# Attention and gated MLP in one kernel: the planner's DMA durations are replaced by traced ones

## Chip, cores and metric

The kernel runs on one core of a Trainium2 chip. The metric is device time in microseconds; the time before is the median of three runs.

## The reference

Causal attention over 4 batches, 12 heads, 448 positions and a head width of 64, in float32; its output is laid out as 1792 tokens of 768 and goes through an MLP with a sigmoid gate.

```python
scores = q @ k.T / 8          # per head, masked above the diagonal with -1e9
attn = softmax(scores)
x = (attn @ v) -> reshaped to (1792, 768)
h = x @ w_in                  # (768, 2048)
g = h * sigmoid(1.702 * h)
out = g @ w_out               # (2048, 768), float32
```

## The kernel before

**Precision.** Most products are made of fp16 pairs: an operand is scaled and split into a high part (`scaled`, L476 on ScalarE or L478 on VectorE) and a rest (`rest`, L481, always VectorE), and three matmuls (high by high, high by rest, rest by high) replace one. The weights arrive as 64-bit numbers (16 loads of `w_in` at L652 and 16 of `w_out` at L704, 768 KB each) and are turned into float32 by the ScalarE and VectorE steps of `to_f32` (L570 to L603) before they are split. Six of the twelve heads' pairs of batch 0 use float32 for scores instead of splits.

**Blocks and units.** The work is cut into 8 blocks: each batch gives rows 0 to 255 (4 chunks of 64) and rows 256 to 447 (3 chunks). A block has 6 units, one for each pair of heads. A unit (`unit`) loads q (L856 for batch 0, L981 otherwise), transposes it (by TensorE at L870 for batch 0, else by a DMA transpose at L1040), makes scores (L1060, L1068), softmax (`chunk`, L1091 on VectorE and L1105 on ScalarE), splits the probabilities into `p`, transposes them by DMA into `PT` (L1179) and multiplies by v (L1197). Keys come at L936 and are transposed by DMA at L961; values come at L780. A `PT` transpose has 12 tiles in a 4-chunk block and 20 in a 3-chunk block; a `qT` transpose has 8 or 6, a `kT` transpose 14.

**MLP.** `h_slice` (L1268) multiplies a block's attention output `xT` by a slice of `w_in` into `ps_h`, gates it (L1289, L1294) and splits it into `gT`. `out_tile` (L1333) multiplies 128 tokens of `gT` by half of `w_out`, scales the result and stores it (L1357). `xT` is held for two blocks; `p`, `PT` and `qT` have two buffers each, `kf` and `qf` one.

**The order of instructions.** Nothing runs as the loops read. Every piece of work is put into a list, `Ops`, with a cost on each engine that can do it, what it reads and writes, a due time (`prio`, from `TUNE`) and, for a DMA, the time `dma` that it takes on the bus. `Ops.order` then simulates the list forward, engine by engine, and takes the order in which the simulation issued; for an operation that two engines can do, it takes the engine too. It repeats this 300 times from one random seed, with due times that a backward simulation yields and that random numbers disturb, and keeps the order with the best simulated score. All DMAs go through the one queue of SyncE. The simulation gives a DMA this time:

```python
go = max([now] + flying[-self.DMA_DEPTH :][: len(flying) // self.DMA_DEPTH][:1])
free[e] = go + costs[e]
bus = max(bus, go + self.DMA_START) + dma
end = bus + self.DMA_END
```

A DMA with `dma` over 1.0 (weights, v, all transposes) is "bulk": it is held back while the simulated bus is more than `TUNE["slack"]`, 5.13 us, behind. `scored` and `late` rate an order with random delays, and use the same constants.

Of the kernel before, what the change touches and what calls it, by code (L numbers as in the profile page):

```python
# [59 lines left out]
class Ops:  # L60
# [9 lines left out]
    HOP = 0.14  # L70
    SECOND = 1e5
    LOAD = 0.68
    DMA_START, DMA_END, DMA_DEPTH = 1.0, 0.8, 8
    ROWS = 0.19

    def __init__(self):
        self.ops = []
# [244 lines left out]
def kernel(  # L322
# [13 lines left out]
    P = 128  # L336
# [25 lines left out]
    vraw = cp.tile([P, NJ, H, D], F32, name="vraw")  # L362
# [411 lines left out]
    def v_batch(b, prio):  # L774
        st = bst[b]
        for j in range(NJ):
            r = min(P, S - j * P)
            add(
                {"SP": Ops.LOAD},
                lambda e, j=j, r=r: nc.sync.dma_start(  # L780
                    out=vraw[:r, j], in_=v[b, :, j * P : j * P + r, :].rearrange("h p d -> p h d")
                ),
                [], [("vraw", j, 0)] + ([("vraw", j, 1)] if r == P else []), prio, dma=2.18 * r / P,
            )
        sqv, sqv_key = col("sqv", 2, 2 * NJ)
        sq, sq_key = col("sqv1", 2)
        if b == 0 and TUNE["gram_v"]:
            x = vraw.rearrange("p j h d -> p j (h d)")
            for j in range(NJ):
                gram(  # L790
                    x[:, j : j + 1], [("vraw", j, h) for h in range(2)], ps_o[1], ("O", 1), j == 0, j == NJ - 1, prio
                )
            gram_max(ps_o[1], ("O", 1), sq, sq_key, prio)
        for j in range(2 * NJ if not (b == 0 and TUNE["gram_v"]) else 0):
            square_sum(
                NU * D, junk(NU * D).rearrange("p (h d) -> p h d", d=D), [],
                vraw[:, j // 2, j % 2 * NU : j % 2 * NU + NU], [("vraw", j // 2, 0), ("vraw", j // 2, 1)],
                sqv[:, j : j + 1], (sqv_key, j), prio,
            )
        if not (b == 0 and TUNE["gram_v"]):  # L800
            add(
                dve(2 * NJ),
                lambda e: nc.vector.tensor_reduce(out=sq, in_=sqv, axis=AX.X, op=ALU.max),
                [(sqv_key, j) for j in range(2 * NJ)], [sq_key], prio,
            )
        amx, amx_key = all_max(sq, sq_key, "v", "S" if b else "O", prio)
        st["s_v"], st["s_v_key"] = col("s_v", 2)
        st["i_v"], st["i_v_key"] = col("i_v", 2)
        norm_scale("v", amx, amx_key, st["s_v"], st["s_v_key"], st["i_v"], st["i_v_key"], prio)
# [41 lines left out]
    def load_heads(dst, src, r, keys, prio, dma):  # L851

        for j in range(2):
            add(
                {"SP": Ops.LOAD},
                lambda e, j=j: nc.sync.dma_start(  # L856
                    out=dst[:r, j], in_=src[j].rearrange("(p t) d -> p t d", p=r)
                ),
                [], keys[j], prio, dma=dma,
            )  # L860
# [16 lines left out]
    def k_unit32(u, c0, c1, prio):  # L877

        m = u % 2
        f = q16[:, m * 16 * D : m * 16 * D + 8 * D].bitcast(F32).rearrange("p (j t d) -> p j t d", j=2, d=D)  # L880
        w = 64 * (c1 - c0)
        r = w // 2
        keys = [("q16", m, j) for j in range(4)]
        load_heads(f, k[0, 2 * u : 2 * u + 2, 64 * c0 : 64 * c1], r, [keys[:2], keys[2:]], prio, 0.045 * (c1 - c0))
        got, got_key = turn(f, r, keys, prio)
        kt = kT[u // 2][:, u % 2 * NC : u % 2 * NC + NC].rearrange("p c w -> p (c w)").bitcast(F32)
        add(
            {**act(w, psum=True, rate=1.2), **dve(w, rate=1.2)},
            lambda e: scaled(e, kt[:, 64 * c0 : 64 * c1].rearrange("p (x t) -> p x t", t=2), got, 1.0),
            [got_key], [("kT", u, c) for c in range(c0, c1)], prio,  # L890
        )
        bst[0]["kT", u] = kt

    def q_unit32(n, u, prio):
        b, c0, c1 = blocks[n]
        ni = c1 - c0
        i = u % 2
        r = 32 * ni
        f = qf[:, i].rearrange("p (j t) d -> p j t d", j=2)
        keys = [("qf", i, j) for j in range(2)]  # L900
        load_heads(f, q[b, 2 * u : 2 * u + 2, 64 * c0 : 64 * c1], r, [[x] for x in keys], prio, 0.045 * ni)
        got, got_key = turn(f, r, keys, prio)
        t = qT_r.next()
        qt = qT[t].rearrange("p c w -> p (c w)").bitcast(F32).rearrange("p (c j w) -> p c j w", j=2, w=64)
        key = ("qT", t)
        if stale[t]:
            stale[t] = False
            for j in range(2):
                add(
                    {"POOL": 0.4},  # L910
                    lambda e, j=j: nc.gpsimd.memset(qt[64 * j : 64 * j + 64, :, 1 - j], 0.0), [], [key], prio - 1,
                )
        for j in range(2):
            add(
                {**act(64 * ni, psum=True, rate=1.0), **dve(64 * ni)},
                lambda e, j=j: scaled(
                    e,
                    qt[64 * j : 64 * j + 64, :ni, j].rearrange("p c (x t) -> p c x t", t=2),
                    got[64 * j : 64 * j + 64].rearrange("p (c x) t -> p c x t", c=ni),
                    1.0,  # L920
                ),
                [got_key], [key], prio,
            )
        return qt[:, :ni], key, -QK_SCALE, None

    def k_pair(b, u, prio):
# [4 lines left out]
        for a in range(2):  # L931
# [29 lines left out]
            lambda e: nc.sync.dma_start_transpose(out=t, in_=flat),  # L961
            [("k16", 0), ("k16", 1)], [("kT", u + a, c) for a in range(2) for c in range(NC)], prio - TUNE["tr"], dma=2 * NC * Ops.ROWS,
        )
# [4 lines left out]
    def q_pair(n, u, prio):  # L968

        b, c0, c1 = blocks[n]  # L970
        ni = c1 - c0
        w = 64 * ni

        f = qf.rearrange("p u c d -> p (u c) d")[:, : 2 * ni]
        keys = []
        for a in range(2):
            for j in range(2):
                keys += [("qf", a, j)]
                add(
                    {"SP": Ops.LOAD},  # L980
                    lambda e, a=a, j=j: nc.sync.dma_start(  # L981
                        out=f[64 * j : 64 * j + 64, a * ni : (a + 1) * ni],
                        in_=q[b, 2 * (u + a) + j, 64 * c0 : 64 * c1].rearrange("(c p) d -> p c d", p=64),
                    ),
                    [], keys[-1:], prio, dma=0.09 * ni,
                )
        sq, sq_key = col("sqq", 2)
        square_sum(
            2 * w, junk(2 * w).rearrange("p (x d) -> p x d", d=D), [], f, keys, sq, sq_key, prio
        )  # L990
        (s, s_key), (inv, inv_key) = col("s_q", 2), col("i_q", 2)
        norm_scale("q", sq, sq_key, s, s_key, inv, inv_key, prio)
        ik, ik_key = bst[b]["ik", u]
        c, c_key = col("c", 3)
        add(
            tiny(1),
            lambda e: by(e).tensor_scalar(
                out=c, in0=inv, scalar1=-QK_SCALE, scalar2=ik, op0=ALU.mult, op1=ALU.mult
            ),
            [inv_key, ik_key], [c_key], prio,  # L1000
        )
        h = q16[:, : 8 * w].rearrange("p (x g h d) -> p x g h d", g=2, h=2, d=D)

        def part(g):
            return [("q16", a, g) for a in range(2)]

        add(
            {**act(2 * w, ap=1), **dve(2 * w, ap=1, rate=0.521)},
            lambda e: scaled(e, h[:, :, 0, 0], f, s),
            keys + [s_key], part(0), prio,  # L1010
        )
        add(
            dve(2 * w, ap=1),
            lambda e: rest(h[:, :, 0, 1], f, s, h[:, :, 0, 0]),
            keys + [s_key] + part(0), part(1), prio,
        )
        for g in range(2):

            def dup(e, g=g):
                dst, src = h[:, :, 1, 1 - g], h[:, :, 0, g]  # L1020
                if e == "DVE":
                    nc.vector.tensor_copy(dst, src)
                else:
                    nc.gpsimd.tensor_scalar(out=dst, in0=src, scalar1=1.0, scalar2=1.0, op0=ALU.mult, op1=ALU.mult)  # L1024

            add({**pool(2 * w, 0.84), **dve(2 * w, rate=0.26)}, dup, part(g), part(2 + g), prio)
        bst[b]["c", n] = c, c_key
# [106 lines left out]
    def unit(n, u, prio):  # L1134
# [15 lines left out]
        for i0 in range(c0 - c0 % 2, c1, 2):  # L1150
# [32 lines left out]
            [("p16", pp_i, x, g) for x in range(ne) for g in range(2)], all_keys, prio - TUNE["tr"],  # L1183
            dma=2 * Ops.ROWS * ne,
        )
# [276 lines left out]
```

## Time and profile before

| | |
|---|---|
| time, median of 3 runs | 640.23 us (637.7 to 640.47) |
| profiled execution | span 633.9 us from the first to the last instruction; its own device time is not listed beside the three runs |
| instructions | 14759 |
| PE busy | 582.6 us, 92% |
| DVE / ACT / POOL busy | 422.4 / 357.2 / 96.6 us |
| SyncE's DMA queue | 62.7% of 16 engines' span |

Read it in stages: an engine's share of the whole span says little, since the first 160 us and the rest have different limits.

### The profile page before, as it was taken

The numbers are of one execution on the slowest core, as the hardware profiler recorded it, in microseconds if no ns is written. First come the engines' busy times: TensorE is split into PE (matmuls) and PEld (weight loads), VectorE is DVE, ScalarE is ACT, GpSimd is POOL, SyncE is SP. The second block draws the span as 40 slices with busy tenths as digits, with TensorE's granted clock in tenths as the row PEclk, the third lists the DMA queues.
The fourth block names the chain that finished last, engine by engine and source line by source line (L and its number), as shares of the span: only waits on it lengthen the run. The fifth ranks groups of instructions, "written<-read, shape, count | busy, mean of one in ns | idle before, by whom it ended". The sixth has DMA issues, their size and how long they took to land. (4 is left out here: it accounts for less than half of the span.)

```text
span 633.9 us, 14759 instructions
## 1 busy us (share of the span) xinstructions
PE 582.6 (92%) x5723; PEld 439.5 (69%) x5723; DVE 422.4 (67%) x1128; ACT 357.2 (56%) x835; POOL 96.6 (15%) x235
## 2 busy tenths in 40 slices
PE   4777688978999999998999999999999999999997
PEld 3555466754588767876678667885679688777964
DVE  4999899999978898977498976769644213101300
ACT  4878888778657776758465565557343223012210
POOL 2233220043202124121021521001000000000000
PEclk9976689999999999999999999999999999999999
DMA  8999969678599687999847798627620040000000
GB/s 276 271 277 293 220 224 284 194 188 166 110 176 190 120 164 124 180 159 173 176 103 135 136 181 160 127 62 130 122 67 2 13 96 1 3 26 26 1 26 26
DMA packets 226407, 85.71 MB, mean 135 GB/s; under 512 B 207137, under 2 KB 216097, under 8 KB 226337
## 3 DMA queue, kind: packets, MB, share of 16 engines
q1 hardware_dynamic: 226336, 84.76, 62.7%
q8 instruction: 45, 0.74, 0.5%
q14 instruction: 26, 0.20, 0.1%
HBM read 41.68 MB, written 5.51 MB: 74 GB/s over the span
## 5 line engine op out<-in xcount | busy, mean ns | idle before, releaser
L1268 PE MATMUL ps_h<-xT,wib 128*128 128x192 f16 (+1 forms) x2304 | 239.3, 261 | 3.5 <-DVE gT L481 3.4
L1333 PE MATMUL ps_o<-wob,gT 128*128 128x384 f16 (+1 forms) x1536 | 233.8, 326 | 5.3 <-DVE wob L481 2.3
L1268 PEld LDWEIGHTS <-wib 128*128 128x128 f16 x2304 | 207.0, 98 | 31.8 <-issue 12.1
L1333 PEld LDWEIGHTS <-gT 128*128 128x128 f16 (+1 forms) x1536 | 131.4, 101 | 87.0 <-issue 12.6
L1105 ACT ACTIVATE z<-z,cols 128x320 f32<-128x320 f32 (+5 forms) x168 | 83.8, 500 | 47.1 <-DVE cols L1091 40.1
L1294 DVE SCALAR_TENSOR_TENSOR ps_h<-t,ps_h 128x512 f32<-128x512 f32 (+1 forms) x64 | 39.9, 624 | 76.5 <-ACT t L1289 76.3
L481 DVE SCALAR_TENSOR_TENSOR p<-z,cols,p 128x384 f16<-128x384 f32 (+3 forms) x168 | 82.6, 523 | 3.0 <-ACT p L476 1.9
L1091 DVE CUSTOM_DVE_ANT_0 z<-ps_s,mask,cols 128x384 f32<-128x384 f32 (+6 forms) x126 | 55.8, 478 | 30.1 <-PE ps_s L1068 30.1
L1289 ACT ACTIVATE t<-ps_h,cols 128x512 f32<-128x512 f32 (+1 forms) x64 | 40.1, 627 | 60.0 <-PE ps_h L1268 59.5
L476 ACT ACTIVATE p<-z,cols 128x128 f16<-128x128 f32 (+3 forms) x108 | 55.3, 538 | 15.4 <-DVE cols L1169 6.7
L1163 POOL TENSOR_SCALAR cols<-cols 128x2 f32<-128x2 f32 (+1 forms) x70 | 20.1, 287 | 208.6 <-ACT z L1105 207.7
L481 DVE SCALAR_TENSOR_TENSOR gT<-ps_h,gT 128x512 f16<-128x512 f32 (+1 forms) x64 | 39.6, 620 | 15.8 <-ACT gT L476 15.7
L476 ACT ACTIVATE gT<-ps_h 128x512 f16<-128x512 f32 (+1 forms) x58 | 31.1, 539 | 28.3 <-DVE ps_h L1294 28.1
L476 ACT ACTIVATE ob<-ps_o,cols 128x384 f32<-128x384 f32 x23 | 13.2, 575 | 59.8 <-PE ps_o L1333 59.8
L1197 PEld LDWEIGHTS <-v 128*64 128x64 f16 x864 | 38.4, 113 | 9.6 <-issue 7.6
L1197 PE MATMUL ps_v<-PT,v 128*64 128x192 f16 (+3 forms) x864 | 41.1, 243 | 4.1 <-DMA PT<-p 4.1
L1068 PE MATMUL ps_s<-kT,qT 128*64 128x192 f16 (+4 forms) x504 | 38.8, 277 | 2.4 <-DVE cols L1091 1.3
L1060 PE MATMUL ps_s<-kT,qT 128*128 128x64 f32 (+6 forms) x84 | 29.3, 468 | 2.6 <-DVE cols L1091 1.9
L1024 POOL TENSOR_SCALAR q<-q 128x512 f16<-128x512 f16 (+1 forms) x30 | 25.2, 841 | 43.0 <-ACT q L476 30.1
L1105 ACT ACTIVATION_READ_ACCUMULATOR z<-z,cols 128x1 f32 x168 | 31.7, 188 | 0.0
L476 ACT ACTIVATE wob<-wob 128x768 f32<-128x768 f32 (+1 forms) x19 | 20.8, 1095 | 15.6 <-DMA wob<-in_moe_w_in_dram 10.6
L1068 PEld LDWEIGHTS <-qT 128*64 128x64 f16 x504 | 19.6, 110 | 13.9 <-issue 9.9
(89 smaller groups left out, 541.1 us busy)
## 6 DMA issues: line engine op xcount, KB each, us to landing
wob<-in_moe_w_in_dram SPq DMA_DIRECT2D x16, 768.0 KB, 6.0
wob<-in_moe_w_out_dram SPq DMA_DIRECT2D x9, 768.0 KB, 5.5
vraw<-in_moe_w_out_dram SPq DMA_DIRECT2D x7, 768.0 KB, 5.4
out_dram<-ob SPq DMA_DIRECT2D x28, 192.0 KB, 2.1
vraw<-in_v_dram SPq DMA_DIRECT2D x12, 384.0 KB, 5.7
kf<-in_k_dram SPq DMA_DIRECT2D x36, 112.0 KB, 2.9
qf<-in_q_dram SPq DMA_DIRECT2D x48, 64.0 KB, 3.2
qf<-in_q_dram SPq DMA_DIRECT2D x48, 48.0 KB, 2.7
```

Of the source, the lines that this page charges most:

```text
L476: nc.scalar.activation(out=dst, in_=src, func=AF.Copy, scale=sc)
L481: nc.vector.scalar_tensor_tensor(out=dst, in0=src, scalar=sc, in1=hi, op0=ALU.mult, op1=ALU.subtract)
L1024: nc.gpsimd.tensor_scalar(out=dst, in0=src, scalar1=1.0, scalar2=1.0, op0=ALU.mult, op1=ALU.mult)
L1060: nc.tensor.matmul(ps, qt[:, i - c0].rearrange("p j w -> p (j w)"), kt[:, : 64 * (i + 1)], start=True, stop=True)
L1068: nc.tensor.matmul(ps[64 * j : 64 * j + 64], qt[:, g, i - c0, 64 * j : 64 * j + 64], kt[:, : i + 1, 64 * j : 64 * j + 64], start=(g == 0), ...
L1091: lambda e: nc.vector.tensor_tensor_reduce(out=z[:, :w], in0=ps, in1=mask[:, S - w :], scale=c, scalar=3.0e38, op0=ALU.add, op1=ALU.min, a ...
L1105: lambda e: nc.scalar.activation(out=z[:, :w], in_=z[:, :w], func=AF.Exp, bias=m, scale=-1.0, accum_out=l),
L1197: nc.tensor.matmul(ps[64 * j : 64 * j + 64, 64 * (first - c0) : w], vt[:, gv, J, j, :], PT[pi][:, at, gp, 64 * j : 64 * j + 64], start=(t ...
L1268: nc.tensor.matmul(ph[:, t], wib[:, sl, u, gw, t * P : (t + 1) * P], xT[x][:, gx, u, :w], start=(u == 0 and gw + gx == 0), stop=(u == NU - ...
L1289: lambda e: nc.scalar.activation(out=th, in_=ph, func=AF.Tanh, scale=ts[:, sl : sl + 1]),
L1294: lambda e: nc.vector.scalar_tensor_tensor(out=ph, in0=th, scalar=1.0, in1=ph, op0=ALU.add, op1=ALU.mult),
L1333: nc.tensor.matmul(po[o : o + m, :OH], gT[:, f, gg, 64 * r : 64 * r + m], wo_pair(f, gw, nh), start=(f == 0 and gg + gw == 0), stop=(f == ...
```

## The change

Durations in the planner's simulation are replaced: the fixed time ahead of a transfer from 1.0 to 1.23 us and behind it from 0.8 to 0.95 us, a tile of a DMA transpose from 0.19 to 0.214 us, a 128-row load of v from 2.18 to 2.43 us, a q or k load of batch 0 from 0.045 to 0.062 us per chunk, a later q load from 0.09 to 0.125 us per chunk. Those of the weights (2.2), later k loads (0.64) and stores (0.6) stay. No instruction, buffer or due time in `TUNE` changes; what can change is the order of instructions on each engine, and which of two engines takes an operation.

```diff
-    DMA_START, DMA_END, DMA_DEPTH = 1.0, 0.8, 8
-    ROWS = 0.19
+    DMA_START, DMA_END, DMA_DEPTH = 1.23, 0.95, 8
+    ROWS = 0.214
...
-                [], [("vraw", j, 0)] + ([("vraw", j, 1)] if r == P else []), prio, dma=2.18 * r / P,
+                [], [("vraw", j, 0)] + ([("vraw", j, 1)] if r == P else []), prio, dma=2.43 * r / P,
...
-        load_heads(f, k[0, 2 * u : 2 * u + 2, 64 * c0 : 64 * c1], r, [keys[:2], keys[2:]], prio, 0.045 * (c1 - c0))
+        load_heads(f, k[0, 2 * u : 2 * u + 2, 64 * c0 : 64 * c1], r, [keys[:2], keys[2:]], prio, 0.062 * (c1 - c0))
...
-        load_heads(f, q[b, 2 * u : 2 * u + 2, 64 * c0 : 64 * c1], r, [[x] for x in keys], prio, 0.045 * ni)
+        load_heads(f, q[b, 2 * u : 2 * u + 2, 64 * c0 : 64 * c1], r, [[x] for x in keys], prio, 0.062 * ni)
...
-                    [], keys[-1:], prio, dma=0.09 * ni,
+                    [], keys[-1:], prio, dma=0.125 * ni,
```

## Rows read from the trace of the kernel before

**Rows 1.** The page: span, busy time, and PE and its granted clock in 40 slices.

```profile
span 633.9 us, 14759 instructions
...
PE 582.6 (92%) x5723; PEld 439.5 (69%) x5723; DVE 422.4 (67%) x1128; ACT 357.2 (56%) x835; POOL 96.6 (15%) x235
...
PE   4777688978999999998999999999999999999997
...
PEclk9976689999999999999999999999999999999999
```

**Rows 2.** By stretch: length; busy PE, PEld, DVE, ACT, POOL; PEclk, DMA share, GB/s.

```profile
0.00:20.00 20.00, 10.53 (x66) 8.28 (x67) 10.65 (x26) 11.46 (x22) 4.91 (x22) 1.00 0.90 280
20.00:100.00 80.00, 60.05 (x504) 45.16 (x505) 74.39 (x178) 66.23 (x138) 22.68 (x39) 0.81 1.01 256
100.00:160.00 60.00, 51.14 (x465) 36.64 (x464) 57.32 (x117) 48.92 (x93) 14.45 (x30) 1.00 0.84 202
160.00:200.00 40.00, 37.04 (x414) 28.76 (x413) 34.41 (x106) 26.13 (x71) 7.34 (x16) 1.00 0.81 153
200.00:300.00 100.00, 98.19 (x1131) 75.36 (x1129) 85.77 (x263) 70.75 (x194) 21.34 (x56) 1.00 0.90 157
300.00:500.00 200.00, 195.36 (x1949) 146.63 (x1949) 138.79 (x409) 108.22 (x278) 25.91 (x73) 1.00 0.58 111
500.00:634.00 134.00, 130.34 (x1203) 98.64 (x1201) 21.07 (x34) 25.51 (x44) 0.00 (x0) 1.00 0.10 26
```

**Rows 3.** DMA issues of the first 100 us: count, KB, median us to landing.

```profile
q<-in_k_dram SPq DMA_DIRECT2D x12, 64.0 KB, 5.1
qf<-in_q_dram SPq DMA_DIRECT2D x12, 64.0 KB, 4.8
q<-in_k_dram SPq DMA_DIRECT2D x12, 48.0 KB, 4.3
qf<-in_q_dram SPq DMA_DIRECT2D x12, 48.0 KB, 5.0
...
PT<-p SPq DMA_TRANSPOSE x7, 7.1
```

**Rows 4.** DMA issues from 200 to 300 us.

```profile
vraw<-in_v_dram SPq DMA_DIRECT2D x3, 384.0 KB, 5.2
qf<-in_q_dram SPq DMA_DIRECT2D x12, 64.0 KB, 2.7
qf<-in_q_dram SPq DMA_DIRECT2D x12, 48.0 KB, 2.2
...
qT<-q SPq DMA_TRANSPOSE x12, 3.2
PT<-p SPq DMA_TRANSPOSE x12, 4.9
vraw<-in_v_dram SPq DMA_DIRECT2D x1, 192.0 KB, 7.1
kT<-k SPq DMA_TRANSPOSE x3, 4.4
```

**Rows 5.** Waits of PE, whole span: total us, times, longest.

```profile
PE ps_o L870 <- DMA q<-in_k_dram: 10.8, 4, 8.4
...
PE ps_v L1197 <- DMA PT<-p: 4.1, 3, 3.0
```

**Rows 6.** Waits of PE from 160 us to the end.

```profile
PE ps_s L1068 <- DMA qT<-q: 1.2, 2, 1.0
PE ps_v L1197 <- DMA PT<-p: 1.2, 2, 0.8
```

**Rows 7.** Waits of ACT in the first 160 us.

```profile
ACT wob L476 <- DMA wob<-in_moe_w_in_dram: 10.6, 7, 3.4
...
ACT wob L476 <- DMA wob<-in_moe_w_out_dram: 5.0, 5, 1.9
```

**Rows 8.** PE's timeline from 72 us: start, duration, operation.

```profile
72.63 3.25 PE L1268 MATMUL ps_h<-xT,wib 128*128 128x256 f16 x18
```

## Prediction

> **What bounds the kernel now.** The page comes first: PE is busy for 582.6 of 633.9 us, and its row of slices shows that what it lacks lies at the left end, where the granted clock falls too [rows 1]. So the kernel has to be read by stretches [rows 2]. From 160 us to the end PE is busy for 37.04 + 98.19 + 195.36 + 130.34 = 460.9 of 474 us at full clock: 13.1 us idle in all, and no order can win more than that there. In the first 160 us it is busy for 121.7 us, idle for 38.3 us, and from 20 to 100 us the mean granted clock is 0.81, that is, part of the time at 1.2 instead of 2.4 GHz. In this stretch VectorE is busy for 74.39 of 80 us and the DMA share is full (1.01): PE waits there for operands that VectorE, ScalarE and the transfers make ready. The MLP's first matmul stands at 72.63 us [rows 8]; before it PE has only attention and small helper matmuls, whatever their order.
>
> The waits tell how much of this is a transfer's doing. Over the whole span PE waits 10.8 us for loads of k and q, 8.4 of them for the first load of all, which nothing can precede, and 4.1 us for PT [rows 5]. From 160 us on, waits for DMAs are 1.2 + 1.2 = 2.4 us [rows 6]. ScalarE waits for weights, 10.6 + 5.0 us early on [rows 7].
>
> **The change part by part.** It adds and removes no instruction and no transfer; every duration of a single instruction keeps its row. What it moves is the order, by what the planner now thinks of DMAs. So the question is whether the new numbers are nearer to the trace, and what follows from the error where they are not.
>
> *A single transfer, late.* From 200 to 300 us the 64 KB q load lands 2.7 us after its issue, the 48 KB one 2.2 us [rows 4]. The planner's old time without a queue is 1.0 + 0.36 + 0.8 = 2.16 and 2.07 us, its new one 1.23 + 0.5 + 0.95 = 2.68 and 2.56 us: nearer for the one, too long for the other. A qT transpose lands in 3.2 us; old 1.8 + 0.19 x 8 = 3.32 or (6 tiles) 2.94 us, new 2.18 + 0.214 x 8 = 3.89 or 3.46 us. A PT transpose lands in 4.9 us; old 1.8 + 0.19 x 12 = 4.08 or (20 tiles) 5.60, mean 4.84; new 4.75 or 6.46, mean 5.60 us. A kT transpose lands in 4.4 us; old 1.8 + 14 x 0.19 = 4.46, new 5.18 us. So for transposes the old numbers fit the late stretch and the new ones are about 0.5 to 0.8 us too long.
>
> *A single transfer, early.* The small loads of the first 100 us land in 4.3 to 5.1 us and PT in 7.1 us [rows 3]. The old numbers without a queue are 1.98 us and 4.08 us, the new ones 2.43 and 4.75 us: both are short of it, and the new ones less so, since the real time contains a full bus. In this stretch the change is toward the trace.
>
> *The bus, early.* In the first 100 us the planner's demand grows by 12 x 2 x 4 x 0.017 = 1.63 us for the 64 KB loads, 12 x 2 x 3 x 0.017 = 1.22 us for the 48 KB ones, (6 x 12 + 20) x 0.024 = 2.21 us for seven transposes [rows 3], and 3.5 x 0.25 = 0.88 us for the v of batch 0 by the code: 5.9 us. The weights themselves keep 2.2 us, but they are bulk and are held while the simulated bus is over 5.13 us behind, so they are what is pushed: in the planner's order their loads, and the conversions on VectorE and ScalarE that follow, stand up to 5.9 us later beside attention work. On the chip the bus was full already, so no byte moves slower; what may come later is the MLP's first matmul. Bounds: nothing, if the order of weights stays, and 5.9 us, if the whole push arrives at PE. From below a gain is not excluded: ScalarE's 15.6 us of waiting for weights [rows 7] can shrink if their users are put later and other work before them. What that can bring is bounded by VectorE's idle time in 20 to 100 us, 80 - 74.39 = 5.6 us [rows 2], because VectorE is what the stretch runs on. I take a loss of half the push, 3.0 us: nothing in the rows tells more of the order, and a VectorE at 93% leaves little to fill.
>
> *The bus, late.* From 200 to 300 us the demand grows by 6 x 32 x 0.024 = 4.61 us for PT (half of each size), 6 x 14 x 0.024 = 2.02 for qT, 3 x 14 x 0.024 = 1.01 for kT, 12 x 0.14 + 12 x 0.105 = 2.94 for q and 0.88 for v [rows 4]: 11.5 us. The traced share there is 0.90 [rows 2], so the planner now sees a bus at about 101% and spreads attention over up to 11.5 us more in this stretch. The work that hides it is the MLP of the blocks before, at PE: it was 98.19 us busy of 100 with attention paced by the old numbers, and the last stretch has 130 us of PE work with the bus nearly empty (0.10) as reserve. Bounds: a gain of the 2.4 us of DMA waits [rows 6] on the one side, 11.5 us on the other, if `xT` of the next block is late where no MLP work is left. I take 0.5 us, the mean of what the idle shares of PE in the rows on either side make of 11.5 us (1.8% from 200 to 300 us: 0.2; 7.4% from 160 to 200 us: 0.85).
>
> *The rest of the edit* (stores and later k loads pay only the longer fixed times, 0.38 us each) is hidden by the same reserve; without cover it would be one such time at the last store, and that one is after the end of planning.
>
> Sum for the span: 633.9 + 3.0 + 0.5 = 637.4 us. The median of the runs stands 6.3 us above the profiled span, so 643.7 us. Half a per cent, 3.2 us, is about what can be told from no change here: the three runs before differ by 2.8 us.
>
> **The rivals.**
>
> *Order changes, time does not* (30%, 640.2 us). For it: 474 of 634 us are PE-bound with 2.4 us of DMA waits, so durations of transfers decide nothing there, and early the bus is full under either set of numbers. Against it: the planner searches with random disturbances and compares scores, so one constant suffices to pick another order and other engine choices in the first 160 us, where 38 us of PE time are open.
>
> *Faster* (29%). The planner now expects the small loads later, puts their users behind other ready work, and ScalarE and VectorE stop waiting in line. If half of VectorE's 5.6 us of idle time is filled, and half of the 2.4 us late, the time is 640.2 - 2.8 - 1.2 = 636.2 us. It decides if more than 3.2 us of VectorE's holes between 20 and 100 us close. Within these 29%, 4% are for more than this: at the full clock the 60.05 us of PE work of that stretch would take 60.05 x 0.81 = 48.6 us, 11.4 us less, and the time would be 628.8 us. That PE waits there on VectorE speaks against it: a shorter matmul then only waits longer. The Trainium skill (TensorE: Matmul & The Clock Gate, section HAM oscillation) states that waits for DMA between bursts of matmuls bring the clock back down each time, so that a removed wait would pay twice; the trace shows the low clock where such waits are, but more of PE's holes there end on VectorE.
>
> *Slower by starvation late* (9%, 640.2 + 11.5 = 651.7 us). Attention, spread by the planner's full bus, hands over `xT` so late that the MLP runs dry; two blocks of `xT` are all the stock there is. From 160 to 200 us PE was 7.4% idle, so the stock can be thin. It decides once PE falls below about 95% between 200 and 500 us. Against it: PE's 98.19 us.
>
> *The change does nothing at all*: only if the search lands on the same order; with every DMA's landing shifted by at least 0.38 us I give it no share of its own; it would end in the 30%.
>
> **How the numbers follow.** The likeliest case is the push of weights early (32%, 643.7 us, by its bounds 640.2 to 646.1 plus the 0.5). With starvation that makes slower 41%, no change 30%, faster 29%. The range reaches below to 640.2 - 5.6 - 2.4 = 632.2 us, all of VectorE's holes early and all DMA waits late, and above to both losses together with two thirds of the late one, 640.2 + 5.9 + 7.6 = 653.7 us; outside lie the clock case and a full starvation. I give 632 to 654 us; the likeliest one's own range is 640 to 647 us.
>
> **What would show it.** Right: the first MLP matmul stands later than 72.6 us, by 1 to 6 us, PE's busy time before 160 us falls below 121.7 us, and from 200 to 500 us PE stays above 97%; waits of PE for qT and PT late fall under 2.4 us, since the planner is now too careful. Wrong step early: the first MLP matmul stands earlier, or VectorE is over 95% busy from 20 to 100 us. Wrong step late: PE below 95% from 200 to 500 us. The forecast is wrong as a whole if the new order differs mostly by chance: then PE's idle time before 160 us moves by several us with no tie to the weights' loads or to DMA waits.

## The result and the profile after

The changed kernel is faster: 628.84 us (median of 4 runs, 628.13 to 629.87) beside 639.23 us (637.7 to 640.47), a ratio of 0.9855 with a 95% interval of 0.982 to 0.9891. The forecast was 643.7 us and slower; the range began at 632.

The page of the changed kernel: span, busy time, PE and its clock in 40 slices, and then the chain that ended last.

```profile
span 626.4 us, 14747 instructions
...
PE 583.0 (93%) x5723; PEld 438.8 (70%) x5723; DVE 415.4 (66%) x1105; ACT 363.5 (58%) x848; POOL 98.3 (16%) x245
...
PE   2767689798999999999999999999999999999997
...
PEclk9967789899999999999999999999999999999999
...
PE 59%; DVE 2%; ACT 0%; issue 0%; DVEq 0%; ACTq 0%
```

PE has the same work as in [rows 1], 583.0 us for 582.6. The 7.5 us between the two spans are PE's holes, and from the second quarter on its row is nines. The chain, where it can be followed back, is nearly all PE's, and no transfer is in it. The profiled run took 628.13 us beside its span of 626.4, so only 1.7 us lie around a span: by that measure the profiled execution of the kernel before took about 635.6 us, some 4.6 us less than its median of 640.23, and the 6.3 us that the prediction put on top of the span were mostly that. So the traces show 7.5 us of the 10.4 us by which the medians differ; the rest is not seen in them.

By stretch, the columns as in [rows 2]:

```profile
0.00:20.00 20.00, 7.21 (x46) 5.48 (x48) 7.50 (x15) 10.76 (x19) 4.52 (x21) 1.00 1.02 263
20.00:100.00 80.00, 60.22 (x510) 45.12 (x507) 77.75 (x187) 68.58 (x142) 23.58 (x41) 0.79 0.97 261
100.00:160.00 60.00, 54.73 (x500) 39.88 (x499) 58.74 (x129) 53.05 (x101) 16.03 (x34) 0.97 0.84 208
160.00:200.00 40.00, 38.66 (x410) 29.08 (x408) 32.66 (x98) 26.06 (x71) 6.98 (x18) 1.00 0.96 177
200.00:300.00 100.00, 99.37 (x1123) 75.71 (x1121) 80.56 (x243) 71.13 (x195) 18.01 (x51) 1.00 0.81 148
300.00:500.00 200.00, 200.00 (x2001) 150.23 (x1999) 136.62 (x402) 109.85 (x281) 29.16 (x81) 1.00 0.61 110
500.00:634.00 134.00, 122.84 (x1149) 93.31 (x1147) 21.57 (x35) 24.03 (x42) 0.00 (x0) 1.00 0.11 24
```

Before 160 us PE is busy for 122.2 us, with [rows 2] 121.7: nothing won, nothing lost. From 160 us to the end it is idle for 626.4 - 160 - 460.9 = 5.5 us, before for 13.0 (633.9 - 160 - 460.9). From 300 to 500 us it has no hole at all, where it had 4.6 us. In both kernels 3.6 us of this idle time lie behind PE's last matmul, while the last results are scaled and stored; what an order could win were the other 9.4 us, and 2.0 us of them are left. So the whole gain lies in the PE-bound stretch, where the prediction put a loss of 0.5 us.

What PE waits for there, first in the kernel before (the longest, beside [rows 6]), then in the changed one, the whole list:

```profile
PE ps_h L1268 <- DVE gT L481: 2.3, 3, 1.4
PE ps_o L1333 <- DVE ob L478: 1.6, 1, 1.6
PE ps_s L1068 <- DVE cols L1091: 1.3, 2, 1.0
```

```profile
PE ps_o L1333 <- DVE wob L481: 1.3, 2, 0.9
PE ps_s L430 <- DVE cols L1091: 0.5, 1, 0.5
PE ps_s L1068 <- DVE cols L1091: 0.2, 1, 0.2
```

No DMA is left in it. The idle time fell by more than the 2.4 us of [rows 6], because transfers also stood further back behind PE's waits. ScalarE's waits for DMAs from 160 us on, in the kernel before (those over 2 us) and then in the changed one:

```profile
ACT waste L466 <- DMA qf<-in_q_dram: 8.5, 8, 2.0
...
ACT k L466 <- DMA kf<-in_k_dram: 5.6, 2, 4.2
...
ACT p L476 <- DMA PT<-p: 2.2, 2, 1.4
...
ACT q L476 <- DMA qT<-q: 2.1, 5, 0.8
```

```profile
ACT waste L466 <- DMA qf<-in_q_dram: 5.6, 5, 2.9
...
ACT q L476 <- DMA qT<-q: 5.6, 4, 2.8
...
ACT k L466 <- DMA kf<-in_k_dram: 0.9, 1, 0.9
```

ScalarE stood in its queue for q and k, and the exponentials, splits and MLP steps behind it were late for VectorE and so for PE. The chain of the kernel before shows such links from a load of q to a wait of PE (for `gT` at 333.57 us, for `cols` at 358.80 us). Start, duration, what:

```profile
325.06 2.24 DMA qf<-in_q_dram
327.40 0.35 ACT waste L466
...
328.01 0.65 ACT z L1105 x2
328.67 0.37 ACT gT L476
329.04 0.55 ACT z L1105 x2
...
333.05 0.48 DVE gT L481
333.57 0.90 PE ps_h L1268 x9
...
343.70 3.18 DMA qf<-in_q_dram
346.99 0.12 ACT waste L466
...
358.21 0.52 DVE z L1091
358.80 0.46 PE ps_s L1068 x4
```

PE stood for 0.60 us before the first of these two matmuls and for 0.95 us before the second. The two longest holes lie ahead of this chain, and the timeline shows the same there. Before the 1.40 us for `gT` that end at 193.34 us, ScalarE had stood for 1.41 us for a PT and then for 0.78 us for a q load, and VectorE's queue behind it. Before the 1.58 us for `ob` that end at 301.41 us, ScalarE had stood for 0.80 us for a load of v, and VectorE then for 2.35 us for ScalarE's `z`, which came behind the work on v, with `ob` behind it in VectorE's queue. How much of each hole the transfer alone made is not told by this (of the last at most 0.80 us). The sum of ScalarE's waits for DMAs is no measure of PE's holes, though: it is 20.0 us here and 12.1 us in the changed kernel, but 19.5 us in `latency`, a run below whose idle time from 160 us on is 7.0 us. So it matters which of them reach PE.

The q loads and the transposes are no faster. From 200 to 300 us in the changed kernel, to be held against [rows 4]:

```profile
qf<-in_q_dram SPq DMA_DIRECT2D x12, 64.0 KB, 2.8
qf<-in_q_dram SPq DMA_DIRECT2D x12, 48.0 KB, 2.3
...
PT<-p SPq DMA_TRANSPOSE x11, 5.0
qT<-q SPq DMA_TRANSPOSE x10, 3.2
```

And the MLP's first matmul is later than in [rows 8], 81.1 us for 72.6 (line, engine, count, duration ns, first and last start):

```profile
L1268 PE MATMUL ps_h<-xT,wib x31: 269/394/421, 81.1 to 89.0; 128*128 128x256 f16 x31
```

### The profile page after: what moved, and what is told of

It is laid out like the page before. It is cut to its first block, busy times and chain, and to the rows that moved or that the text cites. A ratio compares the mean times of both kernels' runs of the same rounds, so it can differ in the third digit from the quotient of the medians.

```text
span 626.4 us, 14747 instructions
## 1 busy us (share of the span) xinstructions
PE 583.0 (93%) x5723; PEld 438.8 (70%) x5723; DVE 415.4 (66%) x1105; ACT 363.5 (58%) x848; POOL 98.3 (16%) x245
## 4 chain that ended last, share of the span: by engine, by line
PE 59%; DVE 2%; ACT 0%; issue 0%; DVEq 0%; ACTq 0%
PE ps_o L1333 28%; PE ps_h L1268 25%; PE ps_s L1068 4%; PE ps_v L1197 3%; DVE z L1091 0%; DVE gT L481 0%; DVE v L481 0%; DVE ps_h L1294 0%; DVE k L481 0%; DVE p L481 0%; DVE p L478 0%; DVE q L481 0%; ACT ob L476 0%; DVE xT L481 0%; PE ps_s L430 0%
## 5 line engine op out<-in xcount | busy, mean ns | idle before, releaser
L1091 DVE CUSTOM_DVE_ANT_0 z<-ps_s,mask,cols 128x320 f32<-128x320 f32 (+6 forms) x126 | 55.9, 478 | 29.3 <-PE ps_s L1068 28.9
L476 ACT ACTIVATE p<-z,cols 128x384 f16<-128x384 f32 (+3 forms) x118 | 60.7, 542 | 14.7 <-DVE cols L1169 13.6
L1163 POOL TENSOR_SCALAR cols<-cols 128x2 f32<-128x2 f32 (+1 forms) x79 | 28.4, 360 | 221.0 <-ACT z L1105 219.8
L1197 PEld LDWEIGHTS <-v 128*64 128x64 f16 x864 | 36.5, 111 | 8.5 <-issue 6.1
L1068 PE MATMUL ps_s<-kT,qT 128*64 128x64 f16 (+4 forms) x504 | 38.7, 277 | 0.2 <-DVE cols L1091 0.2
L1060 PE MATMUL ps_s<-kT,qT 128*128 128x64 f32 (+6 forms) x84 | 30.9, 503 | 6.2 <-ACT qT L476 3.6
L1024 POOL TENSOR_SCALAR q<-q 128x512 f16<-128x512 f16 (+1 forms) x27 | 20.9, 777 | 56.3 <-ACT q L476 47.8
```

Source lines behind the costliest of these rows:

```text
L476: nc.scalar.activation(out=dst, in_=src, func=AF.Copy, scale=sc)
L1060: nc.tensor.matmul(ps, qt[:, i - c0].rearrange("p j w -> p (j w)"), kt[:, : 64 * (i + 1)], start=True, stop=True)
L1068: nc.tensor.matmul(ps[64 * j : 64 * j + 64], qt[:, g, i - c0, 64 * j : 64 * j + 64], kt[:, : i + 1, 64 * j : 64 * j + 64], start=(g == 0), ...
L1091: lambda e: nc.vector.tensor_tensor_reduce(out=z[:, :w], in0=ps, in1=mask[:, S - w :], scale=c, scalar=3.0e38, op0=ALU.add, op1=ALU.min, a ...
L1163: lambda e, ls=ls: by(e).tensor_scalar(out=ls, in0=ls, scalar1=1e-9, scalar2=2.0**-14, op0=ALU.add, op1=ALU.mult),
L1197: nc.tensor.matmul(ps[64 * j : 64 * j + 64, 64 * (first - c0) : w], vt[:, gv, J, j, :], PT[pi][:, at, gp, 64 * j : 64 * j + 64], start=(t ...
```

## The experiments

Two numbers are read from each profile. **Late idle** is the span less 160 us less PE's busy time from 160 us on. **First part** is the span less the late idle, that is, 160 us plus the PE work still to do then; a good start makes it small. Ratios are against the kernel before, timed on the same chip.

| run | transfers of batches 1 to 3 planned | ratio (95%) | span | late idle | first part |
|---|---|---|---|---|---|
| before | old | 1 | 633.9 | 13.0 | 620.9 |
| after | new | 0.9855 (0.982 to 0.989) | 626.4 | 5.5 | 620.9 |
| old_seed3 | old | 0.9994 (0.997 to 1.002) | 632.4 | 12.9 | 619.5 |
| old_seed5 | old | 0.9974 (0.995 to 1.000) | 631.6 | 13.6 | 618.0 |
| new_first | old | 1.0015 (0.999 to 1.004) | 635.8 | 12.3 | 623.5 |
| short_later | shorter | 1.007 (1.003 to 1.011) | 640.0 | 24.6 | 615.4 |
| latency | fixed times new | 0.9861 (0.982 to 0.990) | 623.5 | 7.0 | 616.5 |
| rows | transposes new | 0.9891 (0.986 to 0.992) | 627.9 | 8.5 | 619.4 |
| loads | loads new | 0.988 (0.985 to 0.991) | 627.1 | 8.5 | 618.6 |
| new_seed3 | new | 0.9852 (0.981 to 0.989) | 624.5 | 5.4 | 619.1 |
| new_seed5 | new | 0.9955 (0.992 to 0.999) | 631.6 | 6.2 | 625.4 |
| new_later | new | 0.9821 (0.978 to 0.986) | 621.4 | 5.1 | 616.3 |
| new_later_seed3 | new | 0.9871 (0.983 to 0.991) | 628.4 | 5.6 | 622.8 |
| double | doubled step | 1.0013 (1.000 to 1.003) | 635.6 | 8.3 | 627.3 |
| double_seed3 | doubled step | 1.001 (0.999 to 1.003) | 635.0 | 8.8 | 626.2 |
| double_later | doubled step | 0.9936 (0.992 to 0.996) | 631.0 | 8.4 | 622.6 |
| double_later_seed3 | doubled step | 0.9833 (0.979 to 0.987) | 626.7 | 5.6 | 621.1 |
| hop | old | 0.9865 (0.984 to 0.989) | 627.8 | 10.0 | 617.8 |

**Where it was won: two orders joined.** Both orders are planned, the first 886 of 2845 operations (to about 160 us) are taken from one, the others from the other.

```diff
-        return best[1]
+        head = made[EARLY][:CUT]          # made[0]: old durations, made[1]: new; CUT = 886
+        taken = {i for i, _ in head}
+        return head + [x for x in made[1 - EARLY] if x[0] not in taken]
```

> The first 886 of 2845 operations in the order of the kernel before (about to 160 us), all others in the order and on the engines of the changed kernel. If the gain was made late (PE's idle time from 160 us on went from 13.1 to about 5.5 us, that of the first 160 us stayed at 38 us), the time is within 2 us of the changed kernel's 629, ratio 0.983 to 0.988. If it was made early, it is within 2 us of 639.

> The other way round: the changed kernel's order for the first 886 operations, then that of the kernel before. If the gain was made late: 637 to 641 us, with PE's idle time from 160 us on back at 10 to 14 us. If early: 628 to 631 us.

Neither came out: 635.45 us, ratio 0.9988 (0.9966 to 1.001), and 634.95 us, 0.9979 (0.9954 to 1.0005). The first met a seam. From 160 to 200 us, and its longest late wait of PE (its lines stand 11 further down than the kernel before's):

```profile
160.00:200.00 40.00, 33.23 (x352) 24.52 (x351) 28.79 (x85) 23.11 (x59) 6.83 (x15) 0.91 0.80 163
```

```profile
PE ps_s L441 <- ACT k L477: 5.5, 1, 5.5
```

PE lost 6.8 us at the joint, of which 5.5 in one wait, and the granted clock was 0.91 there. PE's work took 586.6 us, but from 20 to 100 us, ahead of the joint, the clock was lower too (0.77 for 0.81). Behind 200 us the idle time goes with the later order: 4.6 us with the new one (changed kernel 4.2), 8.6 us with the old one (kernel before 10.0). The times are no verdict, the holes only a hint; hence the other way of parting it below.

**Is it a mere draw of the search? Other seeds.**

```diff
-SEED = 2
+SEED = 3          # 3 and 5, with the old and with the new durations
```

> The kernel before with another random seed (3 for 2) and its old durations. If the durations themselves made the gain (an order planned with longer transfers leaves room for them), this stays at 636 to 645 us, with DMA waits of PE late. If the gain was another draw of the random search, this is as likely to be at 629 as at 640.

> The changed kernel with seed 3 for 2. If the durations made the gain: 625 to 632 us, PE's idle time from 160 us on under 8 us, no DMA waits of PE over 1 us there. If it was the draw: anywhere from 628 to 645 us.

> The kernel before with seed 5. If old durations are the cause, 633 to 642 us and about 10 to 15 us of PE idle time from 160 us on, as with seeds 2 and 3 (13.0 and 12.9 us). If a draw can do it, 630 us or less.

> The whole change with seed 5. Theory of room late: 625 to 632 us, PE idle 5 to 8.5 us from 160 us on, as with seeds 2 and 3; the old durations with seed 5 gave a ratio of 0.997 and 13.6 us. A draw: 630 to 640 us.

For the late stretch it is not. Late idle is 13.0, 12.9, 13.6 us with the old durations, 5.5, 5.4, 6.2 us with the new. What the draw moves is the first part: 618.0 to 620.9 us old, 619.1 to 625.4 us new. With seed 5 the draw cost nearly all of the gain; against the same seed with old durations no gain in time can be told (0.9955 beside 0.9974, their intervals overlap). Its time missed the 625 to 632 us expected by 1 us (633.09), its late idle did not.

**One part alone, and twice the step.**

```diff
-    DMA_START, DMA_END, DMA_DEPTH = 1.0, 0.8, 8
+    DMA_START, DMA_END, DMA_DEPTH = 1.23, 0.95, 8     # latency; double: 1.46, 1.1
-    ROWS = 0.19
+    ROWS = 0.214                                      # rows; double: 0.238
-    dma=2.18 * r / P
+    dma=2.43 * r / P                                  # loads; double: 2.68
-    prio, 0.045 * ni)
+    prio, 0.062 * ni)                                 # loads; double: 0.079
-    dma=0.09 * ni
+    dma=0.125 * ni                                    # loads; double: 0.16
```

> Only the fixed times: 1.23 and 0.95 us for 1.0 and 0.8. Theory of the waiting chain (a unit passes a q load, a qT and a PT transpose in turn, and each fixed time that the planner leaves out is met by an engine on the chip): most of the gain, 626 to 630 us beside about 636, PE's idle time from 160 us on 5 to 8 us instead of 13. Theory of the bus (what counts is how full the planner sees it): no gain, 634 to 638 us.

> Only the tile of a transpose, 0.214 for 0.19 us (0.3 to 0.5 us for a PT). Theory of the waiting chain: a third of the gain or less, 632 to 637 us. Theory of the bus: this is two thirds of the late growth of demand (7.6 of 11.5 us between 200 and 300 us), so 627 to 631 us.

> Only the loads of v, q and of batch 0's k. Theory of the waiting chain: little, 633 to 637 us. Theory of the bus: a third of the late growth, 631 to 635 us. These are the durations that the trace of before supports late (2.7 us for a 64 KB q load); if being true is what counts, this is the part that gains most, 627 to 631 us.

> The whole step made twice: 1.46 and 1.10 us, 0.238 us for a tile, v 2.68, batch 0's loads 0.079, q 0.16. If durations gain by being true, this overshoots and gives back, 631 to 640 us. If they gain by leaving room for a transfer that is late, it keeps the gain, 625 to 630 us: too long costs less than too short.

Each part alone gains 1.1 to 1.4%, nearly as much as all three; both theories of the expectations, the waiting chain and the bus, wanted one part to fail. Any of them brings late idle from 13 to 7 or 8.5 us, and it can fall little further: the changed kernel still has 5.5, of which 3.6 lie behind PE's last matmul. These are single seeds, and 4.4, 1.5 and 2.3 us of the shorter spans of `latency`, `rows` and `loads` lie in their first parts. The theory that durations gain by being true had `loads` gain most, which it did not. Its forecast for `double` came out in time (637.59 us, no gain left), yet not by late holes between 200 and 500 us:

```profile
20.00:100.00 80.00, 58.84 (x453) 42.58 (x450) 73.11 (x167) 63.51 (x124) 18.89 (x35) 0.66 0.91 239
...
160.00:200.00 40.00, 35.79 (x347) 24.47 (x347) 33.47 (x93) 26.45 (x63) 11.54 (x25) 1.00 0.82 150
200.00:300.00 100.00, 100.00 (x1144) 77.92 (x1142) 80.52 (x245) 67.74 (x181) 16.17 (x50) 1.00 0.79 147
300.00:500.00 200.00, 199.47 (x2013) 149.89 (x2008) 134.73 (x416) 112.91 (x297) 26.05 (x69) 1.00 0.62 117
```

From 20 to 100 us it gets through 453 matmuls where the kernel before had 504, at a clock of 0.66, with VectorE at 73.11 us and a bus that is no longer full (0.91). That the planner holds back work there that the chip could have done fits this, but the lower clock is part of the loss: PE's whole work took 590.4 us for 582.6. With seed 3, further below, it took only 584.4 us, and the doubled step shows instead as 41.8 us of idle PE in the first 160 us (before: 38.3).

**Which transfers? Batch 0 and the weights, or the rest.** Each transfer carries its own fixed times, so the search runs once, without a seam.

```diff
+def dur(b, old, new):      # weights count as batch 0
+    return LongDur(new) if (b > 0) == (LONG == "later") else Dur(old)
-                bus = max(bus, go + self.DMA_START) + dma
-                end = bus + self.DMA_END
+                bus = max(bus, go + dma.START) + dma
+                end = bus + dma.END
```

> The new durations only for the transfers of batches 1 to 3 and of their stores; those of batch 0 and of the weights keep the old ones. Theory of room late (each longer duration lets the planner put the users of a transfer later in the PE-bound stretch, so fewer of them are met by a late transfer): the whole gain, 625 to 631 us beside about 636, with PE's idle time from 160 us on at 8.5 us or less instead of 13. Theory of the first stretch (loads land late there by over 1 us, so that is where truth pays): no gain, 633 to 638 us. Theory of the mere redraw: either.

> The other half: new durations only for batch 0 and the fixed times of the weights. Theory of room late: no gain, 633 to 638 us, PE idle 10 us or more from 160 us on. Theory of the first stretch: 626 to 631 us.

> New durations for batches 1 to 3 only, seed 3. With seed 2 it ran 1.8% faster than the kernel before, the whole change 1.45%. Theory of room late: 622 to 631 us beside about 636, PE idle under 8.5 us from 160 us on. If leaving batch 0 as it was is an advantage of its own, it also beats new_seed3's ratio of 0.985; if the 1.8% was partly a draw, it lies at 0.982 to 0.99.

PE from 160 us on, first in `new_later`, then in `new_first`:

```profile
160.00:200.00 40.00, 38.72 (x459) 31.33 (x458) 33.44 (x103) 29.59 (x81) 6.08 (x14) 1.00 0.98 168
200.00:300.00 100.00, 99.93 (x1092) 73.78 (x1090) 82.82 (x256) 68.19 (x180) 21.86 (x53) 1.00 0.83 157
300.00:500.00 200.00, 199.83 (x2053) 150.94 (x2052) 137.86 (x408) 111.10 (x288) 24.65 (x72) 1.00 0.62 115
```

```profile
160.00:200.00 40.00, 37.26 (x381) 27.00 (x380) 33.05 (x90) 29.19 (x73) 11.66 (x23) 1.00 0.85 158
200.00:300.00 100.00, 98.67 (x1136) 77.70 (x1135) 88.46 (x274) 68.78 (x188) 19.74 (x52) 1.00 0.80 153
300.00:500.00 200.00, 195.37 (x1960) 146.16 (x1956) 141.26 (x416) 110.89 (x294) 23.64 (x67) 1.00 0.65 116
```

The half for batches 1 to 3 gives the whole gain, 624.46 us and 0.9821; the half for batch 0 and the weights gives none, 637.76 us and 1.0015. `new_later` has the lowest time of the study, with 4.6 us of its span won in the first part, where its durations are the old ones; with seed 3 the first part is 622.8 us, so that share looks like a draw. That leaving batch 0 alone is an advantage of its own is not shown: with seed 3 it has 0.9871 where the whole change has 0.9852.

**The other half of the doubled step.**

> The doubled step only for batches 1 to 3, old durations for batch 0 and the weights. The doubled step everywhere lost the gain although PE was 299.5 of 300 us busy from 200 to 500 us; its loss lay before 200 us (590.4 instead of 583 us of PE time at a lower clock). Theory of room late with a loss early: the gain comes back, 624 to 631 us. If too long a duration costs late as well: 633 us or more.

> The doubled step for batches 1 to 3 only, seed 3. With seed 2 the ratio was 0.9936, a third of the gain of the single step. If too long durations cost late too, it lies at 0.99 to 1.0 again; if that was the draw, at 0.98 to 0.99.

With old durations for batch 0 and the weights the doubled step gains, 0.9936 and 0.9833; with the long ones there too it gains nothing with either seed:

> The doubled step everywhere, seed 3. If too long a duration costs by itself: 632 us or more, with PE over 585 us busy or over 40 us idle in the first 160 us. If seed 2 drew badly: 625 to 631 us.

So most of what doubling costs, it costs in the first stretch: a first part of 627.3 and 626.2 us beside 622.6 and 621.1 us. Whether it costs late as well (late idle 8.4 us with seed 2, 5.6 with seed 3) stays open.

**Dose and kind.** The step taken the other way for batches 1 to 3 (fixed times 0.77 and 0.65, a tile 0.166, v 1.93, q 0.055 us), and old durations with a longer time from any operation to its user:

```diff
-    HOP = 0.14
+    HOP = 0.24
```

> The same step in the other direction, for batches 1 to 3 only: 0.77 and 0.65 us, 0.166 us for a tile, v 1.93, q 0.055. Theory of room late: slower than the kernel before, 638 to 648 us beside about 636, PE idle 15 to 25 us from 160 us on. If any other set of numbers only draws a new order: 626 to 640 us, idle 5 to 14 us.

> All DMA durations old; the planner's time from the end of any operation to the start of one that needs it 0.24 us for 0.14. Theory that the missing room is that behind transfers: late idle time stays at 12 us or more, 633 to 640 us. Theory that room anywhere does it (the old plan met every delay, not only those of transfers): late idle 5 to 9 us, 625 to 632 us.

`short_later` is slower, 641.32 us, 1.007, although its first part is the best of all. Late idle is 24.6 us, and the longest waits of ScalarE and of PE for DMAs are (its lines stand 14 further down):

```profile
ACT waste L480 <- DMA qf<-in_q_dram: 26.6, 14, 6.5
...
PE ps_v L1211 <- DMA PT<-p: 2.3, 5, 0.9
...
PE ps_s L1082 <- DMA qT<-q: 1.6, 1, 1.6
```

`hop` lies between the theories: 0.9865 as the second said, but a late idle of 10.0 us, between both; half of its gain is its first part (617.8 us for 620.9). So in this one seed room that is not tied to transfers helps late, and less.

## Why the prediction was wrong

**The stretches: right.** PE's work stayed at 583 us, and the 13 us of late holes were the bound on a late gain, as it said; 7.5 of them closed. It did not see that 3.6 of them lie behind PE's last matmul and were never to be won.

**The bus, late: the step that failed.** It bounded the gain by "the 2.4 us of DMA waits [rows 6] on the one side" and took a loss of 0.5 us; measured are 7.5 us of gain. The bound counted only waits in which PE itself stood for a transfer. ScalarE stood for transfers too, 8.5 and 5.6 us for q and k, and PE paid some links later under the names of `gT`, `cols` and `ob`: 2.3, 1.3 and 1.6 us, and the chain and the timeline above lead the longest of these waits (0.60, 0.95, 1.40 and 1.58 us) back through ScalarE's queue to a transfer, though not all of each is the transfer's. The Trainium skill (Perfetto Trace Analysis, section Optimization Strategy) says to take the gaps of the engine that bounds, and to find for each the semaphore and the instruction that it waited for. This trace shows that one such link is not enough: it gives 2.4 of PE's 9.4 us of waits to transfers.

The feared price, attention spread by a planner's bus at 101%, did not come: PE was busy for 99.37 of 100 us from 200 to 300 us and then for 200 of 200, as the prediction's own argument on the 98.19 us said. And that the new durations are too long for late transposes was read as a fault. It is harmless there: with `rows`, the part that [rows 4] speaks against, late idle fell by 4.5 us. The dose shows what matters: late idle is 24.6 us with shorter durations, 12.3 to 13.6 with the old (`hop` apart), 5.1 to 6.2 with the new, 5.6 to 8.8 with doubled ones. The reading is that a transfer planned too short makes an engine stand with all that is behind it in its queue, while one planned too long lets other ready work go first. The runs show the dose, and the chain shows the standing; that the users of a transfer are placed later and others before them is argued from the planner's code. The durations also enter the score by which the search picks among its 300 orders, and no run parts that from the placing. The choice of engine is not needed for it: VectorE's load from 200 to 300 us fell from 85.77 to 80.56 us with the change, but with seed 5 it is 88.82 us and late idle falls all the same.

**The bus, early: right in kind, its size open.** It took 3.0 us of loss, within 0 to 5.9, and measured in this pair is 0.0: a first part of 620.9 us in both. The MLP's first matmul did move back, by 8.5 us, more than the 1 to 6 us stated, and PE did as much before 160 us all the same, so its date is no measure of the loss. The push is seen at twice the step: means of 626.8 us for `double` and its seed 3, beside 619.5 us for the old durations with three seeds. At the single step the three seeds give 621.8 us, 2.3 us more: not far from 3.0, but less than they scatter, so that the 0.0 of this pair may be a lucky draw.

**Truth early: no gain.** The small loads are where the new numbers are nearer to the trace, and `new_first`, with one seed, gains nothing by it. That VectorE already was at 93% there would explain it; no run tests that.

**The rivals.** "Faster" had 29% and 636.2 us, with half of VectorE's early holes and half of the late DMA waits. VectorE's holes in 20 to 100 us did close, from 5.6 to 2.3 us, which is more than the 3.2 us that were to decide for this rival, and VectorE was over 95% busy, the prediction's sign of a wrong step early. Yet PE gained nothing there: both signs came true and neither tells why the kernel is faster. Its mechanism, that ScalarE stops waiting in line, is the one that the late stretch shows, but there it counted on only 1.2 us. The clock case did not happen: 0.79 for 0.81 in that stretch. Starvation late: PE is at 100% from 300 to 500 us. A mere draw, named as what would make the forecast wrong as a whole, is refuted for the late stretch and true for the first, where the draw moves the first part by some 7 us (615.4 to 622.8 us among the kernels that plan batch 0 and the weights with old durations).

## What to carry to other kernels

Where a static order is planned from durations, an error in them is not symmetric: in a stretch that one engine bounds, with other work ready, plan transfers rather too long, but not those of a start where the planner would hold back the very work that it runs on (here twice the step cost some 7 us there). Before bounding a gain by an engine's waits for DMAs, look at what the engines that feed it wait for, and follow each hole back to its start. And try two or three seeds of a random search before reading a difference of 1%: here one unlucky draw of the first stretch cost nearly the whole gain.

## What the runs showed of the hardware

Nothing new of a single operation: q loads and transposes landed in the same times before and after, within 0.1 us. Not expected was how evenly the changed kernel runs: 628.13 to 629.87 us in 4 runs, while the kernel before spread from 632.74 to 639.71 us in 25 runs on one chip. That an order with room is also less sensitive to jitter is not shown: the numbers of runs differ, and `latency` and `new_later` spread by 3.8 and 3.6 us in 4 runs each.
